# Attention's end: the order of a multiply, a decode and the token sums on DVE and ACT

## The chip, the cores and the metric

The kernel runs on one core of a Trainium2 chip. The metric is the device time of one execution in microseconds (us). A core has a matrix engine (PE, with its weight loads shown as PEld), a vector engine (DVE), an activation engine (ACT), a general engine (POOL) and a queue engine that issues most transfers (SP). Each engine works through its own instructions in order; semaphores hold an instruction until what it needs is there.

## What is computed

Clustered attention over 2 batches x 8 heads x 768 tokens, then two gated expert layers over the 1536 tokens:

```python
scores = scale * np.matmul(q, k.transpose(0, 1, 3, 2))
scores = np.where(mask, scores, -1000000000.0)      # mask: same nearest centroid
scores = scores - np.max(scores, axis=-1, keepdims=True)
attn = np.exp(scores)
attn = attn / (np.sum(attn, axis=-1, keepdims=True) + 1e-09)
attn_out = np.matmul(attn, v)
# x = attn_out as 1536 x 512
g = x @ w_gate                                       # first layer
x = g * (1 / (1 + np.exp(-g))) * (x @ w_val) @ w_out
gate = 1 / (1 + np.exp(-(x @ moe2_w_gate)))          # second layer
x = gate * (x @ moe2_w_val) @ moe2_w_out
```

All is in float32. The kernel gets float32 precision out of matrix products by splitting each operand into a high part (rounded to a shorter type) and a low part (the rest), and adding three products.

## The kernel before

**Attention** treats 8 pairs of heads (2 batches x 4), each in 12 steps; the loop's time `t` counts steps, so the last pair (7) begins at 84 and U * N = 96 is the end of the softmax passes. A step of `smax` computes scores for the row maxima and sums. Ten steps later `apply` computes the transposed scores `st` (line 520, four matmuls, here called a group), ACT takes their exponential into `pt` (line 525), and `av` multiplies with v into the one PSUM tile `acc` (line 545), two groups at a time, four matmuls for each. The pair's queries come in two halves of 384 (groups 0 to 5 and 6 to 11). After group 5 and after group 11 DVE multiplies `acc` by the reciprocals of the sums, `rbs`, into `hx` (line 551). There is one `acc` and one `rbs`, so the next half has to wait for this multiply. The reciprocals go through small pieces `cc` (lines 495 to 475), a transpose on PE, the copy `R` on ACT (line 505), a transfer by SP into rows of the operand S4l (line 507), and a broadcast on PE with its copy `rbs` on ACT (line 534).

**Order.** A function for each piece of work is put at a time by `add(t, f)`; the loop runs, between the steps' own instructions, all functions whose time has come, so the numbers are the program's order on every engine and no more: no engine looks ahead. Three kinds of such work meet at the end of attention, on DVE and ACT:

- *Weights.* `weights(0, q)` for the first two quadruples of the first expert layer: "g0"/"g1" load 512 KB of raw 64-bit words each, "c0"/"c1" decode them into float32 on DVE (lines 101, 103, 105), "s" makes four sums (line 110), and "x", "y", "z", "w" split them into high parts `th` on ACT (line 118) and low parts `tl` on POOL (line 119). The times are in the table near line 622.
- *Token sums.* The expert layers multiply by Strassen's scheme, which needs the operands S1 to S4 beside A11 to A22 (lines of `hx`: A21 and A22 are the second batch, A12 and A22 the last two pairs). `sums_x(kk, c0, c1, lo_eng)` makes S2 = A22 - S3 and S1 = A21 + A22 in place (lines 557, 558), their high and low parts by `split_x` (line 93 on ACT, line 96 on DVE) and S4 = A12 - S2 (line 561), all in one call. S3 itself is made earlier (line 569), and its parts at `late + 13.47`.
- *The multiply* of line 551, called by `av` at 100.75 and 106.75.

**The expert layers** (`moe`) follow at once. A quadruple is seven products `pa`, `pb`, `pc` (line 686), whose order is written out in `keys`; the first needs A11 and B11, the third S2.

Of the kernel before, what the change touches and what calls it, by code (L numbers as in the profile page):

```python
# [8 lines left out]
F32 = mybir.dt.float32  # L9
# [3 lines left out]
ACTF = mybir.ActivationFunctionType  # L13
ALU = mybir.AluOpType
# [44 lines left out]
def tile_cluster_attention_moe_moe2(  # L59
# [9 lines left out]
    nc = tc.nc  # L69
# [3 lines left out]
    S = NS * 128  # L73
    HB = S // 2
# [9 lines left out]
    X = {nm: tuple(xpool.tile([128, 2, S], F32R, name=f"{nm}{s}") for s in "hl")  # L84
         for nm in ("A11", "A12", "S3", "S1", "S4", "A22", "S2")}
    hx = xpool.tile([128, 4, NT], F32, name="hx")
    A11f, A12f, A21f, A22f = (hx[:, r, c] for c in (slice(0, S), slice(S, NT)) for r in (slice(0, 2), slice(2, 4)))

    def split_x(nm, kk, cs, src, lo_eng, hi_eng=None):

        hi, lo = (t[:, kk, cs] for t in X[nm])
        if hi_eng is None:
            nc.scalar.activation(out=hi, in_=src, func=ACTF.Copy)
        else:
            hi_eng.tensor_copy(out=hi, in_=src)
        lo_eng.tensor_tensor(out=lo, in0=src, in1=hi.bitcast(F32), op=ALU.subtract)
# [69 lines left out]
    def attention():  # L166
        with ExitStack() as st:
# [382 lines left out]
                    t0 = b * S + hb * HB  # L550
                    nc.vector.tensor_tensor(out=hx[:, p, t0:t0 + HB], in0=d["rbs"], in1=acc[:, 0:HB], op=ALU.mult)  # L551

            def sums_x(kk, c0, c1, lo_eng):

                cs = slice(c0, c1)
                x1, x2, x3, x4 = (x[:, kk, cs] for x in (A21f, A22f, A11f, A12f))
                nc.vector.tensor_tensor(out=x3, in0=x2, in1=x3, op=ALU.subtract)
                nc.vector.tensor_tensor(out=x1, in0=x1, in1=x2, op=ALU.add)
                split_x("S2", kk, cs, x3, lo_eng)
                split_x("S1", kk, cs, x1, lo_eng)  # L560
                nc.vector.tensor_tensor(out=x4, in0=x4, in1=x3, op=ALU.subtract)

            def early_x():
                al = slice(0, S)
                P, V = nc.gpsimd, nc.vector
                late = U * (N - 1)

                def s3(kk):
                    V.tensor_tensor(out=A11f[:, kk], in0=A11f[:, kk], in1=A21f[:, kk], op=ALU.subtract)

                for kk in range(2):
                    add(late - 1.4 + kk, lambda kk=kk: split_x("A11", kk, al, A11f[:, kk], P))
                    add(late + 0.6 + kk, lambda kk=kk: split_x("A12", kk, al, A12f[:, kk], P))
                    add(late + 5.2 + kk, lambda kk=kk: s3(kk))
                    add(late + 13.47 + 0.01 * kk, lambda kk=kk: split_x("S3", kk, al, A11f[:, kk], V))
                add(late + 14.3, lambda: sums_x(0, 0, S, V))
                add(late + 19.3, lambda: sums_x(1, 0, HB, V))
                add(late + U + LEAD + 1.5, lambda: sums_x(1, HB, S, V))

            N = len(pairs)  # L580
            U = 2 * NS
            LEAD = 10
# [3 lines left out]
            def add(t, f):  # L586
                at.setdefault(t, []).append(f)
# [34 lines left out]
            add(U * N - 14.2, lambda: (inputs.close(), weight_pools()))  # L622
            for q, when in enumerate((
                {"g0": -14.1, "g1": -14.0, "c0": -9.4, "c1": -8.1, "s": -4.9, "x": -3.9, "y": -3.1, "z": -2.1, "w": -1.1},
                {"g0": -7.0, "g1": -6.0, "c0": 2.5, "c1": 3.5, "s": 4.5, "x": 5.6, "w": 6.1},
            )):
                for k, v in when.items():
                    add(U * N + v, T0[q][1][k])
            early_x()
            due = sorted(at)  # L630

# [347 lines left out]
    with tc.manual_schedule():  # L979
        attention()  # L980
        moe()
# [52 lines left out]
```

## Time and profile before

| | us |
|---|---|
| median of three runs | 845.46 |
| lowest, highest | 844.67, 854.7 |
| the profiled execution | 854.58 |
| its span, first to last instruction | 852.9 |
| PE busy in the span | 819.7 |
| DVE, ACT, POOL busy | 613.7, 444.2, 212.8 |

The profiled execution is one of the longer ones: 9.1 us above the median. The trace gives each instruction's start and length on its engine, and for idle time ahead of it the instruction whose end released it. The chain of waits is followed back from the last instruction. The granted clock of PE is given as a share of 2.4 GHz, so 0.50 is the 1.2 GHz level. Several instructions of one kind in a row are printed merged, with their count (x8) and their time from the first's start to the last's end.

### The profile page before, as it was taken

What the parts mean: (1) busy time and instruction counts of PE and PEld (TensorE: products, weight loads), DVE (VectorE), ACT (ScalarE), POOL (GpSimd) and SP (SyncE); (2) the same over time, 40 slices, a digit from 0 to 9 for tenths busy, and PEclk for the clock granted to TensorE, in tenths of its full rate; (3) what the DMA queues carried; (4) which work ended last, traced back from release to release, by engine and by line L of the source; (5) the groups of instructions that cost most, each with busy time, mean ns of one, the idle gap of its engine ahead of it and who ended that gap; (6) DMA issues with size and microseconds to landing.
All of it is one profiled execution on the core that took longest, in us unless ns stands there. A gap on an engine that the chain in (4) does not pass through costs nothing.

```text
span 852.9 us, 11696 instructions
## 1 busy us (share of the span) xinstructions
PE 819.7 (96%) x4392; PEld 643.1 (75%) x4392; DVE 613.7 (72%) x942; ACT 444.2 (52%) x711; POOL 212.8 (25%) x154
## 2 busy tenths in 40 slices
PE   4699999999999899999999999999999999999997
PEld 1566666666665588888888888888888888888886
DVE  8888777777596667766777999777776776776531
ACT  5577777777788464334436465547334443522231
POOL 7534243143032032333322000313324242200000
PEclk9799999999999899999999999999999999999999
DMA  4663645552530112212122222011211222212021
GB/s 151 180 176 98 176 132 167 132 153 71 137 122 1 50 50 75 75 50 100 52 72 100 75 100 98 1 50 51 74 62 63 76 74 74 101 60 90 24 99 50
DMA packets 26704, 75.43 MB, mean 88 GB/s; under 512 B 4676, under 2 KB 5656, under 8 KB 26648
## 3 DMA queue, kind: packets, MB, share of 16 engines
q1 hardware_dynamic: 26648, 74.69, 28.0%
q8 instruction: 34, 0.56, 0.3%
q14 instruction: 22, 0.18, 0.1%
HBM read 53.51 MB, written 3.15 MB: 66 GB/s over the span
## 4 chain that ended last, share of the span: by engine, by line
PE 90%; DVE 6%; ACT 2%; issue 1%; DMA 1%; SPq 0%; ACTq 0%; DVEq 0%
PE pa L686 24%; PE pb L686 12%; PE st L520 8%; PE acc L545 7%; PE sc L451 7%; PE pc L686 6%; PE pa L820 6%; PE pa L925 6%; PE pc L925 4%; PE pb L820 3%; PE pc L820 3%; PE pb L925 2%; ACT pt L525 1%; DVE cols L457 1%; DMA qkt<-in_qkt_dram 1%
## 5 line engine op out<-in xcount | busy, mean ns | idle before, releaser
L119 POOL TENSOR_TENSOR tl<-w,th 128x512 fp32r<-128x512 f32 x96 | 121.0, 1282 | 366.4 <-ACT th L118 366.3
L457 DVE TENSOR_REDUCE cols<-sc 128x1 f32<-128x768 f32 x96 | 91.3, 953 | 36.2 <-PE sc L451 35.8
L525 ACT ACTIVATE pt<-st 128x768 f32<-128x768 f32 x96 | 77.4, 806 | 56.4 <-PE st L520 56.3
L459 ACT ACTIVATE junk<-sc,cols 128x768 bf16<-128x768 f32 x96 | 85.8, 894 | 7.8 <-DVE cols L457 7.6
L545 PE MATMUL acc<-pt,v 128*64 128x384 f32 x384 | 74.3, 507 | 4.6 <-DVE hx L551 4.1
L707 ACT ACTIVATE u<-pa 128x768 f32<-128x768 f32 x48 | 39.0, 813 | 62.8 <-PE pa L686 62.8
L118 ACT ACTIVATE th<-w 128x512 fp32r<-128x512 f32 x96 | 50.7, 570 | 30.3 <-DVE w L110 30.1
L338 POOL TENSOR_TENSOR nr<-ss,half 128x12 f32<-128x12 f32 x16 | 38.1, 2387 | 90.4 <-DVE ss L336 90.3
L105 DVE SCALAR_TENSOR_TENSOR w<-raw,w 128x512 int32<-128x512 int32 x72 | 51.4, 713 | 2.5
L103 DVE SCALAR_TENSOR_TENSOR w<-raw,w 128x512 int32<-128x512 int32 x72 | 49.9, 693 | 2.5
L707 ACT ACTIVATE p<-pa 128x768 f32<-128x768 f32 x24 | 19.5, 812 | 60.7 <-PE pa L686 60.7
L545 PEld LDWEIGHTS acc<-pt,v 128*64 128x64 f32 x384 | 23.5, 137 | 35.0 <-issue 27.5
L715 DVE TENSOR_TENSOR u<-u,pb 128x768 f32<-128x768 f32 x24 | 22.9, 954 | 33.7 <-ACT u L707 29.8
L110 DVE TENSOR_TENSOR w<-w 128x256 f32<-128x256 f32 x96 | 40.8, 425 | 3.2
L101 DVE TENSOR_SCALAR w<-raw 128x512 int32<-128x512 int32 x72 | 35.0, 486 | 5.6 <-POOL tl L119 5.6
L713 DVE TENSOR_TENSOR hb<-u,pb 128x768 f32<-128x768 f32 x16 | 15.2, 952 | 29.0 <-PE pb L686 18.8
L721 ACT ACTIVATE hb<-hb 128x768 f32<-128x768 f32 x24 | 20.3, 847 | 21.3 <-DVE hb L713 21.3
L520 PE MATMUL st<-S3h,S1h 112*128 112x384 f32 x72 | 26.1, 363 | 1.4 <-ACT pt L525 1.4
L520 PE MATMUL st<-S4h,A22h 112*128 112x384 f32 x72 | 26.3, 366 | 0.6 <-ACT pt L525 0.6
L686 PE MATMUL pb<-S4h,tl 128*128 128x512 f32 x96 | 25.2, 344 | 0.0
L686 PE MATMUL pa<-A11h,tl 128*128 128x512 f32 x96 | 25.2, 344 | 0.0
L686 PE MATMUL pc<-A12h,tl 128*128 128x512 f32 x96 | 25.2, 344 | 0.0
(555 smaller groups left out, 2195.0 us busy)
## 6 DMA issues: line engine op xcount, KB each, us to landing
raw<-in_wgv_dram SPq DMA_DIRECT2D x48, 512.0 KB
raw<-in_wo_dram SPq DMA_DIRECT2D x24, 512.0 KB
qkt<-in_qkt_dram SPq DMA_DIRECT2D x7, 768.0 KB
qkn<-in_tok_dram SPq DMA_DIRECT2D x7, 768.0 KB
v<-in_tok_dram SPq DMA_DIRECT2D x8, 384.0 KB
out_dram<-u SPq DMA_DIRECT2D x6, 256.0 KB
A22h<-kh SPq DMA_DIRECT2D x6, 192.0 KB
S4h<-qh SPq DMA_DIRECT2D x6, 192.0 KB
```

Source lines behind the costliest of these rows:

```text
L105: nc.vector.scalar_tensor_tensor(out=dst, in0=low, scalar=29, in1=dst, op0=ALU.logical_shift_right, op1=ALU.bitwise_or)
L119: nc.gpsimd.tensor_tensor(out=lo, in0=w, in1=hi.bitcast(F32), op=ALU.subtract)
L451: nc.tensor.matmul(out=sc[:, c0:c1], lhsT=o[f"q{j}"][0:r, h, s * 128:(s + 1) * 128], rhs=o[f"k{j}"][0:r, h, c0:c1], start=(j == 1), stop=( ...
L457: nc.vector.tensor_reduce(out=nm, in_=sc[:, 0:S], axis=AX.X, op=ALU.max, negate=True)
L459: nc.scalar.activation(out=junk, in_=sc[:, 0:S], func=ACTF.Exp, bias=nm, accum_out=sums)
L520: nc.tensor.matmul(out=st_[:, h, 0:HB], lhsT=o[f"k{j}"][0:r, h, s * 128:(s + 1) * 128], rhs=o[f"q{j}"][0:r, h, hb * HB:(hb + 1) * HB], sta ...
L525: nc.scalar.activation(out=pt, in_=st_[:, :, 0:HB], func=ACTF.Exp)
L545: nc.tensor.matmul(out=acc[64 * h:64 * h + 64, 0:HB], lhsT=d["v"][:, s, h, :], rhs=pt[:, h, :], start=(s == 0), stop=(s == NS - 1), tile_p ...
L686: nc.tensor.matmul(out=acc[:, c0:c1], lhsT=wt[i][:, kk], rhs=X[x][j][:, kk, c0:c1], start=(start and kk == 0 and ti == 0), stop=(kk == 1 a ...
L707: nc.scalar.activation(out=d[nm], in_=d["a"][:, 0:S], func=ACTF.Copy)
L820: nc.tensor.matmul(out=accs[j][:, c0:c1], lhsT=ws[x], rhs=hs[y][:, c0:c1], start=(k == 0 and ti == 0), stop=(k == KF - 1 and ti == 2))
L925: nc.tensor.matmul(out=accs[j], lhsT=hs[x][:, js], rhs=ws[y], start=(k == 0 and ti == 0), stop=(k == KF - 1 and ti == 2))
```

## The change

The function for the token sums is taken apart: sums, each high part and each low part get times of their own, and so do the high and low parts of S3, which before were made for both indices one after the other. In the table of the second weights, the two decodes, the sums and the first and last split get later times (c0 98.5 to 100.9, c1 99.5 to 101.0, s 100.5 to 102.5, x 101.6 to 104.3, w 102.1 to 105.3), so that the decode stands behind the multiply of the last pair's first half.

```diff
-            def sums_x(kk, c0, c1, lo_eng):
+            def sums_x(kk, c0, c1, t_sum, t_hi2, t_lo2, t_hi1, t_lo1):
                 cs = slice(c0, c1)
+                V = nc.vector
                 x1, x2, x3, x4 = (x[:, kk, cs] for x in (A21f, A22f, A11f, A12f))
-                nc.vector.tensor_tensor(out=x3, in0=x2, in1=x3, op=ALU.subtract)
-                nc.vector.tensor_tensor(out=x1, in0=x1, in1=x2, op=ALU.add)
-                split_x("S2", kk, cs, x3, lo_eng)
-                split_x("S1", kk, cs, x1, lo_eng)
-                nc.vector.tensor_tensor(out=x4, in0=x4, in1=x3, op=ALU.subtract)
+                def sums():
+                    V.tensor_tensor(out=x3, in0=x2, in1=x3, op=ALU.subtract)
+                    V.tensor_tensor(out=x1, in0=x1, in1=x2, op=ALU.add)
+                def hi(nm, x):
+                    nc.scalar.activation(out=X[nm][0][:, kk, cs], in_=x, func=ACTF.Copy)
+                def lo(nm, x):
+                    V.tensor_tensor(out=X[nm][1][:, kk, cs], in0=x, in1=X[nm][0][:, kk, cs].bitcast(F32), op=ALU.subtract)
+                def lo1():
+                    lo("S1", x1)
+                    V.tensor_tensor(out=x4, in0=x4, in1=x3, op=ALU.subtract)
+                for k, f in ((t_sum, sums), (t_hi2, lambda: hi("S2", x3)), (t_lo2, lambda: lo("S2", x3)),
+                             (t_hi1, lambda: hi("S1", x1)), (t_lo1, lo1)):
+                    add(U * N + k, f)
...
-                    add(late + 13.47 + 0.01 * kk, lambda kk=kk: split_x("S3", kk, al, A11f[:, kk], V))
-                add(late + 14.3, lambda: sums_x(0, 0, S, V))
-                add(late + 19.3, lambda: sums_x(1, 0, HB, V))
-                add(late + U + LEAD + 1.5, lambda: sums_x(1, HB, S, V))
+                    hi, lo = (t[:, kk] for t in X["S3"])
+                    add(U * N + (-1.1, 3.3)[kk], lambda hi=hi, kk=kk: nc.scalar.activation(
+                        out=hi, in_=A11f[:, kk], func=ACTF.Copy))
+                    add(U * N + (-0.45, 3.4)[kk], lambda hi=hi, lo=lo, kk=kk: V.tensor_tensor(
+                        out=lo, in0=A11f[:, kk], in1=hi.bitcast(F32), op=ALU.subtract))
+                sums_x(0, 0, S, 1.46, 2.3, 2.4, 2.35, 2.45)
+                sums_x(1, 0, HB, 4.8, 6.3, 6.4, 7.3, 7.4)
+                sums_x(1, HB, S, 11.5, 11.51, 11.52, 11.53, 11.54)
...
-                {"g0": -7.0, "g1": -6.0, "c0": 2.5, "c1": 3.5, "s": 4.5, "x": 5.6, "w": 6.1},
+                {"g0": -7.0, "g1": -6.0, "c0": 4.9, "c1": 5.0, "s": 6.5, "x": 8.3, "w": 9.3},
```

The order on DVE before, from the first index's S1 low part to the multiply of the last pair's first half (`w` is the decoded weights, `raw` their words):

```order
L96 TENSOR_TENSOR S1l<-hx,S1h 128x768
L561 TENSOR_TENSOR hx<-hx 128x768
L101 TENSOR_SCALAR w<-raw 128x2x256
L103 SCALAR_TENSOR_TENSOR w<-raw,w 128x2x256
L105 SCALAR_TENSOR_TENSOR w<-raw,w 128x2x256
L101 TENSOR_SCALAR w<-raw 128x2x256
L103 SCALAR_TENSOR_TENSOR w<-raw,w 128x2x256
L105 SCALAR_TENSOR_TENSOR w<-raw,w 128x2x256
L110 TENSOR_TENSOR w<-w 128x256 x4
L551 TENSOR_TENSOR hx<-rbs,acc 128x384
```

On DVE in the changed kernel, from the second index's S3 low part on, which follows the first index's sums; the sums of lines 557 and 558 are now lines 560 and 561:

```order
L592 TENSOR_TENSOR S3l<-hx,S3h 128x768
L551 TENSOR_TENSOR hx<-rbs,acc 128x384
L560 TENSOR_TENSOR hx<-hx 128x384
L561 TENSOR_TENSOR hx<-hx 128x384
L101 TENSOR_SCALAR w<-raw 128x2x256
L103 SCALAR_TENSOR_TENSOR w<-raw,w 128x2x256
L105 SCALAR_TENSOR_TENSOR w<-raw,w 128x2x256
L101 TENSOR_SCALAR w<-raw 128x2x256
L103 SCALAR_TENSOR_TENSOR w<-raw,w 128x2x256
L105 SCALAR_TENSOR_TENSOR w<-raw,w 128x2x256
L567 TENSOR_TENSOR S2l<-hx,S2h 128x384
L110 TENSOR_TENSOR w<-w 128x256 x4
```

The multiply now precedes both decodes and the weight sums; one S3 low part (of the second index) stays ahead of it, the other has gone ahead of the reciprocals' pieces.

On ACT before, from the copy of the first `rbs` to the last exponential of attention:

```order
L534 ACTIVATE rbs<-rb 128x384
L525 ACTIVATE pt<-st 128x768 x2
L118 ACTIVATE th<-w 128x512
L534 ACTIVATE rbs<-rb 128x384
L118 ACTIVATE th<-w 128x256
L525 ACTIVATE pt<-st 128x768 x2
L93 ACTIVATE S2h<-hx 128x384
L93 ACTIVATE S1h<-hx 128x384
L525 ACTIVATE pt<-st 128x768 x2
```

And on ACT in the changed kernel, the same stretch:

```order
L534 ACTIVATE rbs<-rb 128x384
L590 ACTIVATE S3h<-hx 128x768
L525 ACTIVATE pt<-st 128x768 x2
L534 ACTIVATE rbs<-rb 128x384
L525 ACTIVATE pt<-st 128x768
L564 ACTIVATE S2h<-hx 128x384
L525 ACTIVATE pt<-st 128x768
L564 ACTIVATE S1h<-hx 128x384
L525 ACTIVATE pt<-st 128x768
L118 ACTIVATE th<-w 128x512
L525 ACTIVATE pt<-st 128x768
```

The second weights' first split (`th`, 128x512) has moved from ahead of the second `rbs` to directly ahead of the last exponential, and the second S3 high part now stands behind the first `rbs`.

## Rows read from the trace of the kernel before

**Rows 1.** The page: the span, and the engines' shares of the chain ended last.

```profile
span 852.9 us, 11696 instructions
...
PE 90%; DVE 6%; ACT 2%; issue 1%; DMA 1%; SPq 0%; ACTq 0%; DVEq 0%
```

**Rows 2.** Busy time by stretch: length, then PE, PEld, DVE, ACT, POOL, clock, DMA.

```profile
40.00:45.00 5.00, 5.00 (x17) 4.53 (x17) 4.91 (x7) 2.92 (x6) 3.48 (x3) 0.50 0.93 198
280.00:283.20 3.20, 0.03 (x2) 0.06 (x2) 3.00 (x7) 0.71 (x2) 0.82 (x1) 0.58 0.75 236
283.20:287.40 4.20, 4.20 (x13) 2.26 (x14) 1.93 (x2) 1.41 (x3) 1.21 (x2) 0.50 0.17 68
292.40:840.00 547.60, 547.60 (x2990) 471.29 (x2989) 391.01 (x546) 238.72 (x338) 114.37 (x90) 1.00 0.19 68
```

**Rows 3.** Chain of waits, 269 to 293 us: start, length, engine, tile, line.

```profile
282.48 0.56 DVE hx L551
...
283.17 2.83 PE acc L545 x8
286.00 2.25 PE st L520 x8
288.25 1.44 PE acc L545 x8
289.69 0.91 PE st L520 x4
...
290.68 0.82 ACT pt L525
...
292.41 0.78 PE pa L686 x3
```

**Rows 4.** Timeline of PE, 268 to 284 us: start, length, instruction, [idle before <-releaser].

```profile
270.50 1.51 PE L545 MATMUL acc<-pt,v 128*64 128x384 f32 x8
271.94 0.45 PE L520 MATMUL st<-S4h,A22h 112*128 112x384 f32 x1
...
274.42 0.45 PE L520 MATMUL st<-S4l,A22l 99*128 99x384 f32 x1
...
276.03 0.87 PE L545 MATMUL acc<-pt,v 128*64 128x384 f32 x4 [0.38 <-ACT pt L525]
276.83 0.45 PE L520 MATMUL st<-S4h,A22h 112*128 112x384 f32 x1
...
278.75 0.33 PE L520 MATMUL st<-S4l,A22l 99*128 99x384 f32 x1
283.17 1.54 PE L545 MATMUL acc<-pt,v 128*64 128x384 f32 x4 [4.09 <-DVE hx L551]
```

**Rows 5.** Timeline of ACT, 262 to 300 us, the same columns.

```profile
269.97 1.57 ACT L93 ACTIVATE S3h<-hx 128x768 fp32r<-128x768 f32 x2
271.44 0.46 ACT L505 ACTIVATE R<-rp 12x384 fp32r<-12x384 bf16 x1
...
275.19 0.79 ACT L525 ACTIVATE pt<-st 128x768 f32<-128x768 f32 x1
...
281.67 0.63 ACT L118 ACTIVATE th<-w 128x512 fp32r<-128x512 f32 x1 [2.95 <-DVE w L110]
```

**Rows 6.** Timeline of DVE, 266.5 to 284.2 us, the same columns.

```profile
269.05 0.21 DVE L475 TENSOR_TENSOR cc<-cols,cc 128x12 bf16<-128x12 f32 x1
270.84 1.83 DVE L96 TENSOR_TENSOR S3l<-hx,S3h 128x768 fp32r<-128x768 f32 x2 [1.58 <-ACT S3h L93]
...
277.06 0.42 DVE L101 TENSOR_SCALAR w<-raw 128x512 int32<-128x512 int32 x1
...
280.76 1.80 DVE L110 TENSOR_TENSOR w<-w 128x256 f32<-128x256 f32 x4
...
283.06 1.04 DVE L557 TENSOR_TENSOR hx<-hx 128x384 f32<-128x384 f32 x1
```

**Rows 7.** Timeline, 303 to 330 us: the third weights' decode on DVE.

```profile
308.15 0.43 DVE L101 TENSOR_SCALAR w<-raw 128x512 int32<-128x512 int32 x1 [3.10 <-POOL tl L119]
```

## The prediction

> **What bounds the kernel now.** I read the page first: PE carries 90% of the chain that ended last and DVE 6% [rows 1]. The busy times by stretch show where these shares lie. From 292.4 to 840 us PE is busy for all of the 547.6 us at a granted clock of 1.00 [rows 2], so the expert layers are bound by PE, and a microsecond won or lost ahead of 292.41 us (the first expert product, end of [rows 3]) reaches the end of the kernel one for one, unless the expert layers get a new wait. The one large hole ahead of that is at the change: from 280.0 to 283.2 us PE works 0.03 of 3.20 us [rows 2].
>
> The timeline of PE gives the hole its size and name. The last score group before it ends at 278.75 + 0.33 = 279.08 us, and the next attention x v product starts at 283.17 after an idle time of 4.09 us, released by DVE's multiply on line 551 [rows 4]. There is one PSUM tile `acc`, so the second half of the last pair can't begin to accumulate until line 551 has read the first half. That first half was complete at 276.03 + 0.87 = 276.90 us [rows 4], but line 551 runs only at 282.48 [rows 3]: it stands on DVE behind the token sums and the decode of the second weights, which begins at 277.06 and whose last part runs from 280.76 [rows 6].
>
> The hole has an after-effect. The granted clock averages 0.58 in it and is 0.50 from 283.2 to 287.4 us [rows 2], the 1.2 GHz level; PE had been idle before it fell and had worked for about 4.2 us when it came back. In that time eight `acc` products take 2.83 us where the next eight take 1.44, and eight score products take 2.25 us where four take 0.91 soon after [rows 3].
>
> **The change, part by part.** Nothing is added or removed in arithmetic: the same instructions run in another order on DVE and ACT; PE's order is unchanged.
>
> *Line 551 ahead of the decode.* What stands in front of it on DVE is now the token sums of the first index and the second S3 low part. To see whether it is late again I follow the chain from 269.05 + 0.21 = 269.26 us, where the last reciprocal pieces end [rows 6]; nothing ahead of that is later than now, as the first S3 high part now goes into a gap in which ACT waits for PE, at about 265.4 us. If it did not fit there, one ACT activation of about 0.8 us (1.57 for two [rows 5]) would be the price; I take 0.
>
> On ACT, the two S3 high parts (1.57 us from 269.97) leave the front of `R`, so `R` starts at about 270.0 in place of 271.44 [rows 5]. The exponential of score group 4 follows when PE has finished that group at 270.50 [rows 4]; with 0.8 us for each activation, it ends at about 271.4, S2 high at 272.2, S1 high at 273.1, and the exponential of group 5 can run from 273.1 to 273.9 instead of from 275.19 [rows 5]. DVE's sums, which those high parts need, begin at 269.3 and no longer wait for ACT's S3 high parts, as the low parts do now for 1.58 us from 269.26 to 270.84 [rows 6]. So PE no longer waits for the exponential of group 5 (now 0.38 us before the product at 276.03 [rows 4]). The rows of `R` also reach group 6 about 1.4 us sooner, and PE's waits for that transfer inside group 6 (the four matmuls run from 273.22 to 274.42 + 0.45, some 0.5 us more than a group's 0.91) go away. Products 4 and 5 then start at about 274.1 and end at 275.55. Group 7 starts there, against 276.83 now [rows 4]: **1.3 us**.
>
> DVE meanwhile: S2 low from 272.2, S1 low, the A12 sum, each 0.9 to 0.95 us, to 275.0; S3 low of the second index after its high part on ACT (exponential 5, `rbs` at about 0.5, S3 high at 0.84: ready at about 275.2), to 276.2; line 551 from 276.2 to 276.8. PE gets to its next `acc` product only after groups 7 and 8 with the reciprocals' broadcast, which take 276.83 to 279.08 = 2.25 us now [rows 4], so at 275.55 + 2.25 = 277.80. Line 551 is early by 1.0 us, and the wait of **4.1 us** goes.
>
> *No hole, so no fall of the clock.* With PE working through, the eight `acc` products take 1.44 and not 2.83, two score groups 2 x 0.91 and not 2.25 [rows 3]: 1.39 + 0.43 = **1.8 us**.
>
> *What the moved decode makes late.* This is the new risk. The high part of the second weights' first split (line 118) is behind the decode, and on ACT the exponential of the last score group now stands behind it; before, six activations followed this split, and it was done long before them. Its time: line 551 ends at 276.8, two half sums at about 0.55 (as the 0.56 of line 551 for the same size [rows 3]) bring 277.9, the decode 280.76 - 277.06 = 3.70 [rows 6] brings 281.6, one half-size low part 282.1, two of the four weight sums (1.80 / 4 each [rows 6]) 283.0, the split itself 0.63 [rows 5] 283.6. PE: `acc` products from 277.80 to 279.24, groups 9 and 10 to 281.06, `acc` to 282.50, group 11 to 283.41. So the last exponential starts at 283.4 to 283.6: the split is in its way by 0.2 us at most, and less if neighbours on DVE overlap, as they do in the trace. I take 283.5 against 290.68 now [rows 3]. What follows, 292.41 - 290.68 = 1.73 us [rows 3], is the same instructions as now.
>
> **Sum.** 290.68 - 283.5 = 7.2 us, and the parts agree: 1.3 + 4.1 + 1.8 = 7.2. The expert layers start at 285.2 instead of 292.41.
>
> *The other moves cost nothing.* The split's low part on POOL would be done near 285 us and is first read by the second quadruple, five products of 2.12 us after the start. The next weight loads on SP are released by the decode's reads of the raw tiles, now some 0.5 us later in absolute time; their decode waits today for POOL's split and not for a transfer (3.10 us at 308.15 [rows 7]), so the loads have room. The sums of the last half keep their distance to the last `acc` product, with the weights' half-size low parts and adds on DVE ahead of them done by about 284.9, before that product ends.
>
> **Bounds.** A matter the trace can't show is how far the new order really lets the chain run. The smallest gain I can argue is the wait alone, 4.1 us (the clock falls for another reason, group 7 no earlier). The largest is PE without any gap: were the last exponential covered too, the last eight `acc` products would end at 283.41 + 1.44 = 284.85 and not at 285.2, so 7.6.
>
> **Against which time.** The profiled execution took 854.58 us (span 852.9 [rows 1]), 9.1 us above the median of the runs, 845.46, and equal to the highest of the three, 854.7. Its sum gives 854.58 - 7.2 = 847.4. The other two runs, 845.46 and 844.67, were without something that this trace has; the clock is also 0.50 from 40 to 45 us with PE busy throughout [rows 2], far ahead of the change, so I take the difference to arise at least partly before it and to stay. The likeliest median is 845.46 - 7.2 = **838.3 us**.
>
> **The rivals.**
> *The clock did not fall in the two faster runs.* Then they lost only the wait and the lateness of group 7, 4.1 + 1.3 = 5.4 us, and the median is 840.1. For it: this trace is the slower level. Against it: PE stands idle for 4.09 us in every run, since DVE's order is fixed, and the one trace there is shows the fall. The Trainium skill ("TensorE: Matmul & The Clock Gate", Part 1: The HAM clock gate) says that the monitor's windows run free of the kernel, so that the same kernel sees its clock change at different places from run to run. By that rule some runs would keep the full clock over the hole; no run here shows one that did.
> *The median falls on the upper level.* The whole gain is there, but two of three runs are of the kind profiled: 847.4. The runs shown are split two to one the other way.
> *A new wait takes part of the place.* Line 551 late behind S3 low, or the split in front of the last exponential: each us by which DVE is later than worked out costs 1 us. With 2 to 3 us, the smallest-gain bound of 4.1, it is 841 to 842. Against it: 1.0 us of slack for the first. For it: nearly none for the second.
> *Slower.* The one mechanism is the split ahead of the last exponential. An add on DVE that meets POOL's work took 1.04 us instead of 0.56 [rows 6]. Were all of the 6.8 us from line 551 to the split doubled, the split would end at 290.4, the last exponential would start about where it does now, and PE would have stood for 7 us; the clock would fall and cost some 2 us as now: 845.5 - 0.3 + 2 = 847. It decides from about 5 us of delay. Against it: POOL has nothing to do between 266 us and the split itself.
> *The change does more.* Over 2% means 16.9 us; the whole stretch from 270 to 292 us holds no such time. Only a comparison in which the kernel before sits on the upper level and the changed one on the lower (854.6 against 838.3, 1.9%) comes near.
>
> **How the numbers follow.** Chances: the forecast 0.52 (its own range 837.5 to 841), no fall of the clock in the faster runs 0.17, the upper level 0.15, a part of the gain lost 0.09, slower 0.03, more than 2% 0.04. The range takes in the largest gain (837.9), a run's scatter of some 0.8 us (845.46 to 844.67) below it, and the upper level: 837 to 848. A difference of about 2% is what a measurement of this kernel can tell from no change; the forecast is 0.9%. So within 2%: 0.95, faster 0.04; the slower case itself stays within 2%, and I leave 0.01 for slower.
>
> **What would show it.** In the changed kernel's trace: no idle time of PE before `acc` released by line 551; clock 1.00 from 270 us on; `R` at about 270.0, exponential 5 at about 273.1, group 7 at 275.6, line 551 at about 276 (before 277.8), the last exponential at 283.4 to 283.6, the first expert product at about 285.2, and 560.5 us from there to the end as now. A wait of ACT for the weight sums that PE then shares, or idle time in the second and third quadruple, would prove it wrong; so would a start of the expert layers at 287 or later.

## The result and the profile after

The changed kernel took 840.88 us (median of 4 executions, 839.95 to 842.74). The kernel before, with one execution more than its table has, took 849.62 (4 executions, 844.67 to 854.7). The ratio is 0.986 with a 95% interval from 0.982 to 0.991: faster by 1.4%, within the 2% band. The profiled execution took 839.95 us, with a span of 838.2.

These medians hide that both kernels have groups of executions. Over the whole study the kernel before ran 94 times: 36 executions took 844.6 to 849.3 us and 58 took 851.7 to 858.4. The changed kernel ran 22 times: 6 at 837.9 to 840.0, 11 at 840.7 to 842.7 and 5 at 846.8 to 847.7. So a median of three or four says mostly which group it fell into, and the change itself has to be read from the traces. The times agree with them when like groups are compared: the lowest group has a median of 838.5 us against 845.9 before (the 22 executions below 847), the highest 847.3 against 855.1, so 7.4 and 7.8 us.

The page of the changed kernel, and its busy times by stretch (columns as in [rows 2]):

```profile
span 838.2 us, 11695 instructions
...
PE 91%; DVE 5%; ACT 2%; DMA 1%; issue 1%; SPq 0%; ACTq 0%; DVEq 0%
```

```profile
262.00:280.00 18.00, 17.72 (x91) 10.36 (x91) 13.36 (x23) 15.70 (x27) 3.30 (x3) 1.00 0.01 1
280.00:285.00 5.00, 5.00 (x28) 2.70 (x24) 4.83 (x10) 3.33 (x6) 0.69 (x1) 1.00 0.56 175
...
292.00:830.00 538.00, 538.00 (x2977) 467.13 (x2976) 387.82 (x539) 235.48 (x333) 115.30 (x90) 1.00 0.20 69
```

Where [rows 2] had 0.03 us of PE work in 3.20 us, PE is now busy for all of 280 to 285 us, and the granted clock is 1.00 in each of these stretches, from 262 us on. The chain of waits through the same place shows it piece by piece (start, length, engine, tile, line):

```profile
276.89 0.90 PE st L520 x4
277.79 0.36 PE rb L531
278.15 0.91 PE st L520 x4
279.06 1.44 PE acc L545 x8
280.50 1.61 PE st L520 x8
282.12 1.44 PE acc L545 x8
283.56 0.91 PE st L520 x4
...
284.55 0.82 ACT pt L525
...
286.28 2.28 PE pa L704 x12
288.56 2.08 PE pc L704 x12
```

No piece is on DVE any more: line 551, which stood in this chain before [rows 3], is gone from it. The eight `acc` products take 1.44 us each time, and two groups in a row (280.50, x8) take 1.61 us, against 2.25 in [rows 3].

This execution was 1.27 us late ahead of the change: the last reciprocal piece on DVE (line 475) stands at 270.32 and not at 269.05 [rows 6]. The first S3 parts, which now run ahead of it, are not the cause: in the chain of waits the eight `acc` products ahead of these parts already start at 264.40 and not at 263.13, 1.27 us later too, and the S3 high part (266.55 to 267.40) ends before ACT's next exponential, at 267.50, which waits for PE. Times of the two are compared below with these 1.27 us taken off. DVE and ACT (start, length, instruction, idle time before it and its releaser):

```profile
270.32 0.21 DVE L475 TENSOR_TENSOR cc<-cols,cc 128x12 bf16<-128x12 f32 x1
...
277.10 0.55 DVE L551 TENSOR_TENSOR hx<-rbs,acc 128x384 f32<-128x384 f32 x1
...
278.63 0.42 DVE L101 TENSOR_SCALAR w<-raw 128x512 int32<-128x512 int32 x1
...
282.69 1.80 DVE L110 TENSOR_TENSOR w<-w 128x256 f32<-128x256 f32 x4
284.40 1.63 DVE L567 TENSOR_TENSOR S1l<-hx,S1h 128x384 fp32r<-128x384 f32 x1
```

```profile
271.25 0.46 ACT L505 ACTIVATE R<-rp 12x384 fp32r<-12x384 bf16 x1
...
274.27 0.81 ACT L525 ACTIVATE pt<-st 128x768 f32<-128x768 f32 x1
...
283.60 0.64 ACT L118 ACTIVATE th<-w 128x512 fp32r<-128x512 f32 x1 [0.23 <-DVE w L110]
```

Line 551 runs at 277.10, before the decode begins at 278.63. PE's next `acc` product starts at 279.06, so the multiply, which ends at 277.65, is 1.4 us early. From line 475 to the first expert product it was 292.41 - 269.05 = 23.4 us; it is 286.28 - 270.32 = 16.0 us. **Attention's end became 7.4 us shorter; 7.2 were forecast.**

The spans differ by more, 852.9 - 838.2 = 14.7 us. Of this, 7.4 is attention's end, and the later start takes 1.3 back. The other 8.6 us are in the expert stage, in which no instruction was changed and PE waits for nothing in either trace: 852.9 - 292.41 = 560.5 us before, 838.2 - 286.28 = 551.9 us after. The last row above, 2.08 us for twelve matmuls, is where it comes from; in the trace of before the same product and the next one read:

```profile
294.73 2.12 PE pc L686 x12
296.85 2.12 PE pa L686 x12
```

Each product of twelve matmuls took 2.12 us there and takes 2.08 here, at a granted clock of 1.00 in both, and so until the last projection begins, some 450 us later. The experiments had to tell whether that is the change's doing.

### The profile page after: what moved, and what is told of

Read it like the earlier page. It is cut to its first block, busy times and chain, and to the rows that moved or that the text cites. A ratio compares the mean times of both kernels' runs of the same rounds, so it can differ in the third digit from the quotient of the medians.

```text
span 838.2 us, 11695 instructions
## 1 busy us (share of the span) xinstructions
PE 805.3 (96%) x4392; PEld 638.4 (76%) x4392; DVE 614.5 (73%) x942; ACT 444.4 (53%) x711; POOL 214.1 (26%) x154
## 4 chain that ended last, share of the span: by engine, by line
PE 91%; DVE 5%; ACT 2%; DMA 1%; issue 1%; SPq 0%; ACTq 0%; DVEq 0%
PE pa L704 24%; PE pb L704 12%; PE st L520 8%; PE sc L451 8%; PE acc L545 7%; PE pc L704 6%; PE pa L838 6%; PE pa L943 6%; PE pc L943 4%; PE pb L838 3%; PE pc L838 3%; PE pb L943 2%; ACT pt L525 1%; DVE cols L457 1%; DMA qkt<-in_qkt_dram 1%; PE rb L531 1%
## 5 line engine op out<-in xcount | busy, mean ns | idle before, releaser
L520 PE MATMUL st<-S3l,S1l 99*128 99x384 f32 x72 | 25.1, 349 | 0.0
L704 PE MATMUL pa<-A11h,th 128*128 128x512 f32 x96 | 24.6, 336 | 0.0
L704 PE MATMUL pb<-S1h,th 128*128 128x512 f32 x96 | 24.5, 336 | 0.0
```

The source lines that it names most:

```text
L520: nc.tensor.matmul(out=st_[:, h, 0:HB], lhsT=o[f"k{j}"][0:r, h, s * 128:(s + 1) * 128], rhs=o[f"q{j}"][0:r, h, hb * HB:(hb + 1) * HB], sta ...
L704: nc.tensor.matmul(out=acc[:, c0:c1], lhsT=wt[i][:, kk], rhs=X[x][j][:, kk, c0:c1], start=(start and kk == 0 and ti == 0), stop=(kk == 1 a ...
```

## The experiments

In each, "the way" is the time from line 475 on DVE to the first expert product in the profiled execution (by the timeline: 23.29 us before, 15.89 changed), since it doesn't depend on the start or on the expert stage.

### The two halves of the change

Only the table of the second weights, on the kernel before:

```diff
-                {"g0": -7.0, "g1": -6.0, "c0": 2.5, "c1": 3.5, "s": 4.5, "x": 5.6, "w": 6.1},
+                {"g0": -7.0, "g1": -6.0, "c0": 4.9, "c1": 5.0, "s": 6.5, "x": 8.3, "w": 9.3},
```

> The kernel before with only the second weights' table changed (decode, sums and splits at the new times); token sums and S3 parts in one call each, as before. Theory: the multiply of line 551 then runs as soon as the first index's sums are done, at about 277.1 us on the scale of the kernel before, so PE's 4.1 us wait and the clock's fall (1.8 us) go; but the sums of the second index's half now stand behind the decode, and their high parts on ACT in front of the exponential of group 10, so that PE waits near the end: expert layers start near 288, gain 4 to 5 us of the 7.2 of the whole change. Rival (the token sums' order is worth nothing): gain 7 us, the same as the changed kernel.

The way was 18.25 us: 5.0 of the 7.4 us. Eleven of 12 executions took 849.2 to 851.5 us and one 840.6; the ratio to the kernel before is 0.996 (0.991 to 1.000). Line 551 is early, the hole is gone and the granted clock is 1.00 in every stretch from 275 us on, but two small waits of PE take its place, as expected. DVE, ACT and PE in this kernel:

```profile
276.87 0.55 DVE L551 TENSOR_TENSOR hx<-rbs,acc 128x384 f32<-128x384 f32 x1
...
282.76 0.55 DVE L557 TENSOR_TENSOR hx<-hx 128x384 f32<-128x384 f32 x1
```

```profile
283.34 0.53 ACT L93 ACTIVATE S2h<-hx 128x384 fp32r<-128x384 f32 x1 [1.26 <-DVE hx L557]
...
284.24 0.79 ACT L525 ACTIVATE pt<-st 128x768 f32<-128x768 f32 x1
```

```profile
285.09 0.87 PE L545 MATMUL acc<-pt,v 128*64 128x384 f32 x4 [0.81 <-ACT pt L525]
286.31 0.87 PE L545 MATMUL acc<-pt,v 128*64 128x384 f32 x4 [0.35 <-ACT pt L525]
```

The sums of the last half (line 557) come behind the decode, at 282.76; the S2 high part waits for them on ACT for 1.26 us, with the exponential of group 10 behind it; PE waits 0.81 and then 0.35 us for exponentials. So the move of the decode needs the token sums taken apart: that is worth the other 2.4 us.

Only the token sums and S3 in steps, the decode where it was (the changed kernel with the old table line):

> The changed kernel with the second weights' table as before, so that the decode stands ahead of line 551 again; token sums and S3 parts in steps as in the change. Theory: group 7 starts 1.3 us earlier, but PE's wait for line 551 (about 4 us) and the fall of the clock after it stay: gain 1 to 1.5 us. Rival (the order of the sums carries the gain): 7 us. On the time per expert product (twelve matmuls: 2.12 us in the profiled execution of before, 2.08 in that of the changed kernel): if the hole with its fall of the clock is what leads to 2.12, some executions of this kernel show the higher level, 8 to 9 us above the others; if the change's order of the sums brings 2.08, none do.

The way was 21.72 us, a gain of 1.6. PE:

```profile
274.67 0.44 PE L520 MATMUL st<-S4h,A22h 112*128 112x384 f32 x1
...
280.89 2.83 PE L545 MATMUL acc<-pt,v 128*64 128x384 f32 x8 [3.97 <-DVE hx L551]
...
284.77 0.34 PE L520 MATMUL st<-S4l,A22l 99*128 99x384 f32 x1
```

The wait for line 551 is still there (3.97 us), and the eight products after it take 2.83 us. Executions: 10 of 12 at 852.2 to 854.6, one at 843.8 and one at 847.5; the ratio is 0.998 (0.994 to 1.002). Both theories of the order were right in their part: the sums' order alone brings the earlier group 7, and the hole needs the decode moved.

### What the fall of the clock costs

The kernel before with matmuls that nobody reads in the hole:

```diff
+            def fill():
+                fp = ps_sc.tile([128, 1024], F32, tag="sc", name="fp")
+                for s in range(FILL):
+                    nc.tensor.matmul(out=fp[:, 0:512], lhsT=X["A11"][0][:, 0, 0:128], rhs=X["A11"][0][:, 0, 0:512],
+                                     start=True, stop=True)
+
+            FILL = 18
+            add(U * N + 6.4, fill)
```

> The kernel before, with 18 more matmuls of 128x512 (about 0.21 us each at the full clock, 3.9 us) on PE in the hole, into a spare PSUM tile that nothing reads; DVE and ACT as before. Theory: the wait stays, the clock does not fall, so eight acc products take 1.44 instead of 2.83 and two groups 1.8 instead of 2.25: gain 1.8 us over an execution of the kernel before at the same time per expert product. Rival (the clock's fall costs nothing beyond the wait, or PE is held by something else after the wait): no change. On the time per expert product: if the fall of the clock leads to 2.12 us, all executions show 2.08; if it is drawn anew in each execution whatever stands ahead, both levels show.

PE of this kernel, and two stretches of its busy times:

```profile
278.91 4.26 PE L632 MATMUL fp<-A11h 128*128 128x512 f32 x18
283.10 1.51 PE L545 MATMUL acc<-pt,v 128*64 128x384 f32 x8
```

```profile
281.00:283.00 2.00, 2.00 (x10) 1.47 (x8) 1.90 (x5) 0.63 (x1) 0.63 (x1) 1.00 0.88 234
283.00:285.00 2.00, 2.00 (x12) 0.95 (x12) 1.97 (x3) 1.50 (x3) 1.43 (x2) 1.00 0.41 160
```

The clock stays at 1.00. The `acc` products still start at 283.1, when line 551 is done, but now take their ordinary 1.5 us. The way was 21.27 us, 2.0 less than before, against 1.8 expected. All six executions took 843.5 to 844.9 us, with 2.08 us per expert product in the profile.

The price of the fall is not the same in each execution. A second profile of the kernel before:

> The kernel before once more, for a second profile. Four times of it lie in two groups, 844.7 to 845.5 and 853.8 to 854.7. Theory: the groups differ in the time per expert product, 2.08 against 2.12 us, 264 products' worth of PE work from 292 us on (8.6 us), and not in attention; a profile of the lower group then has the same hole and 2.08. Rival: the groups differ ahead of 292 us (the clock at 20 to 45 us), and the time per product is 2.12 in every execution of this kernel.

```profile
280.00:282.60 2.60, 0.00 (x0) 0.01 (x1) 2.43 (x7) 0.66 (x2) 0.77 (x1) 0.90 0.78 241
282.60:285.50 2.90, 2.88 (x9) 0.97 (x9) 1.99 (x2) 1.46 (x3) 1.27 (x2) 0.50 0.29 110
```

Here the clock was still at 0.90 in the hole and at 0.50 only until 285.5 us; the way was 22.71 us, 0.6 less than in the first profile, with the same wait of 4.1 us. In a third profile with the same hole (e8_before_one, below) the mean is 0.51 over the 10.5 us from 282.0 on, and the way was 25.75 us:

```profile
278.00:282.00 4.00, 1.21 (x5) 0.70 (x5) 3.79 (x8) 1.00 (x2) 0.00 (x0) 1.00 0.41 125
282.00:292.50 10.50, 9.19 (x27) 4.87 (x28) 4.70 (x8) 4.26 (x8) 2.03 (x2) 0.51 0.17 55
```

Against the 21.27 us of e3_fill, in which the clock does not fall, the fall costs 1.4 us in the second profile, 2.0 in the first and somewhat over 4 in the third (some 0.2 us of whose 25.75 are an added matmul). The fall is not what leads to 2.12 us per product: e1_decode_only has none and 2.12, e8_before_one has the longest and 2.08. As to the groups of executions, the profiled execution of e4_before was of the slower group again (853.46 us, 2.12 us per product), so it did not show a faster one; the run's ten executions lay in both (845.0 to 857.4).

### The time per expert product

The changed kernel again, beside the kernel before on one chip, and a third time on another:

> The changed kernel once more, on one chip with the kernel before. In the profiled executions the way from the last reciprocal piece (line 475) to the first expert product is 23.3 us before (22.7 in its second profile) and 15.9 changed, and the expert stage takes 560.5 us at 2.12 us per product or 551.9 at 2.08. Theory: the change is worth 7 to 7.4 us within one level, so against the lower group of before (845 to 847) it is at 838 to 840, and its four times so far (839.95 to 842.74) were of the lower level with a start that was 1.3 us later; if the level is drawn anew in each execution with the odds of the kernel before, about two in three executions lie near 847. Rival: the change fixes the level at 2.08, and all executions lie within 3 us.

> The changed kernel once more, on the same chip as the two others, for its odds: theory, executions in groups near 838.5 to 840 (2.08 us per product throughout), near 842 (2.08 until the fourth product of the second layer and 2.12 from there on) and near 847 (2.12 throughout). Rival: one group only on this chip, which would make the level a matter of the chip and not of the execution.

The first gave 841.4, 841.8, 842.1 and 847.1, 847.3, 847.6 us, a ratio of 0.989 (0.984 to 0.994); the second 5 executions at 837.9 to 839.4, 5 at 841.3 to 841.5, and 846.8 and 847.7, a ratio of 0.988 (0.985 to 0.992). So the rival of one level for the changed kernel and that of one group for a chip are both out: the group is drawn in each execution, and three groups exist on one chip. The profile of 841.8 us shows the middle one. Its expert stage begins with 2.08 us per product and changes in the middle (chain of waits from the ninth product of the second layer on):

```profile
576.56 2.08 PE pa L704 x12
578.64 2.17 PE pb L704 x12
580.81 2.12 PE pa L704 x12
```

One product takes 2.17 us, and all from there on take 2.12. Counted in twelves of matmuls it is the layer's tenth; the expectation above calls it the fourth. At this place, 293.4 us into the stage, all nine profiles with 2.08 us ahead of it (after, e3, e5 to e9, e11, e12) have one start-to-start step between matmuls of 0.27 to 0.29 us where 0.23 is usual; the five with 2.12 (before, e1, e2, e4, e10) have none. In two of the nine (e5, e12) 2.12 us follows.

If the rhythm is what PE's stream brings into the expert stage, something small in front of it should change the odds. With one matmul more, behind attention's last product, they were others:

```diff
+            def one():
+                fp = ps_sc.tile([128, 1024], F32, tag="sc", name="fp")
+                nc.tensor.matmul(out=fp[:, 0:128], lhsT=X["A11"][0][:, 0, 0:128], rhs=X["A11"][0][:, 0, 0:128],
+                                 start=True, stop=True)
+
+            add(U * N + 11.2, one)
```

On the kernel of e1_decode_only:

> The kernel of e1_decode_only (11 of 12 executions at the higher level) with a single matmul of 128x128 (under 0.1 us) on PE between attention's last product and the first expert product. Theory: the time per expert product (2.12 or 2.08) is a rhythm in which PE's stream of weight loads and matmuls leaves attention, and which nothing breaks afterwards, as PE never waits again; then a shift of a tenth of a microsecond at the entry can flip it, and the odds of the two levels change clearly from 1 in 12. Rival: the level comes from something else in an execution (memory, the chip, other engines' work), and the odds stay near 1 in 12.

Five of six executions took 840.2 to 842.7 us and one 849.0, where 11 of 12 had been at 849 to 851. The entry in the chain of waits:

```profile
288.30 0.26 PE fp L631
288.56 2.13 PE pa L692 x12
290.69 2.08 PE pc L692 x12
```

The added matmul costs 0.26 us in the chain, but the first product takes 2.13 instead of 2.32 us, and the next 2.08 instead of 2.12. On the changed kernel and on the kernel before:

> The changed kernel with the same single matmul ahead of the first expert product. Theory of the entry rhythm: the odds may change from the changed kernel's own (all of four at 2.08), with executions 8 to 9 us longer. Rival: no effect, all at 2.08, and a time within 0.3 us of the changed kernel.

> The kernel before with the same single matmul ahead of the first expert product. Theory of the entry rhythm: the share of executions at the lower level (about one in three for the kernel before) changes clearly; if to all, the kernel before would be at 845 to 847 with the hole still there, and the changed kernel's gain over it only the 7 us of attention's end. Rival: one in three, as before.

The first gave six executions at 837.9 to 839.0 us, a median of 838.05 and a ratio of 0.981 (0.977 to 0.985) to the kernel before: shorter than both kernels. The second gave 5 of 12 at 845.0 to 846.3, 3 at 847.7 to 848.8, 3 at 850.2 to 850.9 and one at 853.8, where the kernel before beside it had 9 of 17 at 854.5 to 858.4; the odds changed, though not to one group: 11 of 12 lay below 851 us, and 8 of 17 without the added matmul. Length and place of the added matmul:

> The changed kernel with one matmul of 128x512 (0.2 us at the full clock) ahead of the first expert product, where e7_after_one had one of 128x128 and all six executions lay at 837.9 to 839.0. Theory: a full-width weight load and matmul in front of the first expert product puts PE's stream into the 2.08 us rhythm, whatever its length; all executions then lie at 838 to 839.2, 0.15 us above e7_after_one. Rival: what counts is the shift in time, and another length brings the executions at 847 back in part.

> The changed kernel with the 128x128 matmul of e7_after_one one place earlier, ahead of attention's last eight acc products and not behind them. Theory: the last entry counts, and between this matmul and the first expert product there are the acc products with their wait for the last exponential, as in the changed kernel; the odds are those of the changed kernel (of its 10 executions 3 at 847.1 to 847.6, 7 at 840.0 to 842.7), the time otherwise the same within 0.3 us. Rival: one full-width matmul anywhere behind the last score group is enough, and all lie at 838 to 839.

With 512 columns instead of 128: 837.9, 838.7, 839.0, 841.4, 846.7 and 848.2 us, so the rival's outcome came, two of six near 847 as against 5 of 22 without it, and a full-width matmul at the entry is not by itself enough. With 128 columns, but ahead of the last eight `acc` products (`add(U * N + 10.6, one)`): all 12 executions at 846.4 to 848.3. That is neither expectation: neither the changed kernel's odds nor 838, but, by the times, 2.12 us in every execution:

```profile
283.77 0.07 PE fp L649
...
285.59 2.31 PE pa L710 x12
287.90 2.12 PE pc L710 x12
```

A matmul that takes 0.07 us of the chain, with attention's end otherwise as in the changed kernel (the way is 15.9 us in both), comes with every execution in the slowest of the changed kernel's groups, 9 us above its fastest; on the same chip e11_after_third had 2 of 12 there. How it does this is not shown. The timeline of PE has the last score group ahead of the added matmul:

```profile
282.79 0.44 PE L520 MATMUL st<-S4h,A22h 112*128 112x384 f32 x1
...
283.43 0.34 PE L520 MATMUL st<-S4l,A22l 99*128 99x384 f32 x1
283.61 0.22 PE L649 MATMUL fp<-A11h 128*128 128x128 f32 x1
```

The steps between the starts of this group are already those that go with 2.12 us in the other kernels (below, under what stays open), so in this execution the slower rhythm was there before the added matmul ran.

The best version once more:

> The kernel of e7_after_one (the changed kernel with one matmul of 128x128 ahead of the first expert product) once more, as the candidate for the best version. Its six executions lay at 837.9 to 839.0, while the changed kernel's 22 lay in three groups (6 at 837.9 to 840, 11 at 840.7 to 842.7, 5 at 846.8 to 847.7). Theory: the extra matmul makes the 2.08 us rhythm sure, also behind the wait in the second layer, and all executions lie within 838 to 840. Rival: six of six was luck or that chip's, and groups near 841.4 or 847 turn up.

One execution at 839.2, five at 841.1 to 842.5; median 841.83, ratio 0.986 (0.983 to 0.990). By their times all 12 executions of the two runs of this kernel had 2.08 us in the first layer, but not all in the second: the profile of 842.1 us has 2.12 from the tenth product of the second layer on. None of the 12 lay in the group at 847, against 5 of 22 of the changed kernel, which is too few to call that group avoided; otherwise the extra matmul is no gain over the changed kernel.

## Why the prediction was right, and where it was not

**The wait of PE (4.1 us): right.** `acc` no longer waits for line 551. It was forecast to run at 276.2, with the later start taken off it ran at 275.83; its slack was 1.4 us and not 1.0, since in the trace neighbouring activations and adds start before the one ahead has ended (on DVE 0.95 us long and 0.87 apart), where the forecast laid them end to end.

**Group 7 earlier (1.3 us): right.** Less the 1.27 us: `R` at 269.98 (forecast 270.0), exponential 5 at 273.00 (273.1), group 7 at 275.6 (275.55). e2_sums_only, which has this part alone, gained 1.6: 1.3 from group 7, which starts 6.49 us behind line 475 and not 7.78, and the rest in a slightly shorter wait and a slightly cheaper fall of the clock.

**No fall of the clock (1.8 us): right, for the execution profiled.** e3_fill, which keeps the hole and fills it, gained 2.0. The 0.2 us more, in it and in the change (7.4 and not 7.2), have their place: two score groups in a row take 1.61 us, where the sum took 2 x 0.91. The term is one draw of several: the way is 22.71 to 25.75 us in three profiles with the same hole. The rival in which the clock does not fall in some executions was not seen in any trace with the hole unfilled (four profiles: the two of before, e2, e8). The times fit a fall in most of them: on the chip of e3_fill eleven executions of the kernel before took 845.0 to 846.9 us, median 845.87, and the six of e3_fill have 844.08, 1.8 less. A single execution without the fall is not excluded.

**The split in front of the last exponential: right, and as tight as forecast.** The split began at 283.60 and PE's group 11 ended at 284.47; the exponential followed at 284.55, held up by PE. That is 283.28 on the scale of before, forecast 283.4 to 283.6. The slower rival, a split late by some 5 us, had no ground. The slow adds beside POOL's work that it drew on did occur, but behind the split: the S1 low part at 284.40, with POOL busy from 284.31 on, took 1.63 us.

**The other moves: no cost, as forecast.** There is no idle time of PE in 292 to 830 us.

**Wrong: the expert stage "as now", and with it the account of the two levels.** The prediction took the 9.1 us between the profiled execution and the median to arise "at least partly" ahead of the change, from the clock at 40 to 45 us. The trace of the changed kernel has 0.50 there too. The traces of before and after differ by 8.6 us in the expert stage, 2.12 against 2.08 us per product, from the first product to the last projection. No faster execution of the kernel before was profiled, so that its own two groups differ in the same way is inferred, from e3_fill and e8_before_one: both keep its hole and have 2.08 us, and their profiled times are 844.0 and 848.6. Starts do differ between executions, by up to 2.1 us (line 475 at 268.18 to 270.32 in the profiles). That the median lies within 2.6 us of the forecast (840.88 against 838.3) is partly luck: by their times three of the four executions were of the middle group, whose profile in e5 has an expert stage 3.0 us longer, and none of the upper one. The number alone is nearer to the rival without the fall of the clock (840.1); it is the traces that speak for the forecast. The rival with the upper level, 847.4, is met by 5 of the 22 executions (846.8 to 847.7). For the odds of the groups the prediction had only three executions, and the change turned out to shift them: 5 of 22 at the upper level, where the kernel before had 58 of 94 in its upper group. This is why the ratio, 0.986, is further from 1 than 7.2 us of 845 (0.991). That shift can't be put down to the multiply's new place: with it alone (e1_decode_only) 11 of 12 are at the upper level, and one unread matmul goes with a shift either way.

**What stays open.** What in PE's stream makes the two rhythms was not found. It is there already in attention: in the last score group the steps between the four matmuls' starts are 277 to 278, 179 and 178 to 179 ns in before, e1, e2, e4 and e10, and 280 to 281, 176 to 177 and 176 to 177 in after, e3, e5, e7, e9, e11 and e12; the first set goes into 2.12 and the second into 2.08 us. In e6 the group has the first set, and 2.08 follows behind the added matmul; in e10 it has the first set ahead of the added matmul. So a small change of the program goes with another rhythm; by which rule, and whether an added matmul does it by running or by making the program another, stays open. Nor is it shown what the late step in the second layer is for.

## What to carry to other kernels

A cheap read that frees the only copy of an accumulator belongs ahead of any long work on its engine that nobody waits for yet; following the chain by hand from rows of the trace gave its worth to 0.2 us, against the execution whose trace was read; another fall of the clock makes it 6.8 us (from the way of e4_before) or 9.7 (e8_before_one against e7_after_one). When such work moves, look at which in-order queue then has its consumer: here the decode's move alone gave two thirds (5.0 of 7.4 us), because the last token sums and their high parts came behind it. And before a difference of 1% is read from medians, compare the stage that wasn't touched: here it differed by 8.6 us, more than the change was worth.

## What was not expected of the hardware

At the same granted clock of 1.00, the same matmuls and weight loads ran at two steady rates, 2.12 and 2.08 us for twelve matmuls (128x512 and 128x256 in turn, each with its weight load), in most profiles for some 450 us without change. By the groups of times the rate differs from execution to execution of one program, on each of the chips used, and in these traces it holds from the second product on and changes only at a step that is about 0.05 us late in the second layer. With one added matmul of 128x128 all 12 executions of a kernel were, by their times, at one rate; with the same matmul in another place of another kernel 5 of 6 were at the other, where 1 of 12 had been. The cause was not found.
